# The order of TensorE's attention matmuls in the four middle blocks of an attention and two-layer MoE kernel: from a list schedule to the order of emission

## The chip, the cores and the metric

The kernel runs on one core of a Trainium2 chip. The metric is the device time of one execution in microseconds (us); lower is better. Five engines work in parallel, each through its own instruction stream in order: TensorE (PE) multiplies matrices, VectorE (DVE), ScalarE (ACT) and GpSimd (POOL) do elementwise work, SyncE (SP) issues DMAs. An instruction waits for what it needs, and everything behind it in its stream waits too.

## What is computed

Attention over q, k, v of shape (4, 8, 576, 64), then two feed-forward stages over 2304 tokens:

```python
def _attn_ref(q, k, v):
    ...
    out_d = sm_attn(q_d, k_d, v_d)          # q, k, v averaged over groups of 4 tokens
    out_up = np.repeat(out_d, factor, axis=2)
    mask = np.abs(pos[:, None] - pos[None, :]) < factor
    ...
    out_local = np.matmul(attn, v)          # softmax over the band |i - j| < 4
    return out_up + out_local

def _moe_ref(x, w_gate, w_val, w_out, rms_g):
    xn = x / rms * rms_g
    g = xn @ w_gate
    silu = g * (1.0 / (1.0 + np.exp(-g)))
    return silu * (xn @ w_val) @ w_out

def _moe2_ref(x, w_in, w_out, s, b):
    r = np.maximum(x @ w_in, 0.0)
    return (s * (r * r) + b) @ w_out
```

## The kernel before, in words

The 2304 tokens are cut into 8 **blocks** of 288. A block of the first feed-forward stage is `main(blk)`: 12 pairs of accumulations `pg` and `pvl` (gate and value), 12 matmuls of 128x288 each, then 4 output rows `po` of 36 matmuls each. The generator yields after every 12 matmuls, so a block has 36 **steps**. Before it, attention must be there: batch b of the attention gives blocks 2b and 2b+1. Blocks 0 and 1 run together (`main01`), while batch 1 of the attention is computed beside them. Batch 2 is computed beside blocks 2 and 3, batch 3 beside blocks 4 and 5. Blocks 6 and 7 run beside the preparation of the second stage's weights, and the second stage (`ph`, `y`) follows.

A batch of attention is four **units** (one pair of heads each), written as the generator `attn_unit`. In the before a new unit starts every `UNIT_STEP` = 10 steps of the block. A unit does, in this order: load `qkf` and `vd`, `vw` (q, k; v in groups of 4; v in windows); sums of squares and their sum over partitions on TensorE, `ss`; from it powers of two as scales (`pow2`); `qk`, high and low halves of q and k (ACT, then DVE); a DMA transpose to `qkT`, from which DVE copies `q_b`; `pd` (24 small matmuls on `qk`), its halves `qd` and six copies `qd_b`; `sd` (9 matmuls) and the softmax to `P_d`, whose DMA transpose is `PdT`; `sl` (27 matmuls, in two parts) on `q_b` and `qkT` and the softmax to `P_l`, whose DMA transpose is `PlT`; `vh` and `vdh`, halves of v (POOL, ACT, POOL); `pvd` (36 matmuls, waits for `PdT`), `pl` (30 and 24 matmuls, wait for `PlT` and `vh`), their sum into X, and squares into `sq_sum`. After the four units `norm` makes `ssn` and `rb` for each half of the batch and scales X.

Buffers couple the units. `qkf`, `qk`, `qkT`, `P_l`, `PlT` have one buffer each. `vd` and `vw` share one buffer (tag "vd"), so the order in which the code asks for them is the order in which they take turns. `ss`, `pd`, `sd`, `ssn` and `rb` share one PSUM buffer (tag "x"), `pvd` and `pl` another (tag "v"). The accumulations of `main` have four ("mm"), that is two pairs. All DMAs of the units go through SP's one stream.

In the before the framework's list schedule places each instruction of each engine by its priority and by when it holds it to be ready; `main` steps and one step of the attention are emitted in turn. So TensorE's stream splits the attention's matmuls and sets pieces of several units side by side.

Of the kernel before, what the change touches and what calls it, by code (L numbers as in the profile page):

```python
# [35 lines left out]
UNIT_STEP = 10  # L36
# [35 lines left out]
def kernel(  # L72
# [197 lines left out]

    def softmax_d(sd, scale, de=None):
        dm = ap.tile([128, 3], F32, tag="dm", name="dm", bufs=2)
        dz = ap.tile([128, 3], F32, tag="dz", name="dz", bufs=2)
        dve.tensor_reduce(out=dm, in_=sd, axis=AX.X, op=ALU.max)
        dve.tensor_scalar(out=dm, in0=dm, scalar1=scale, scalar2=-1.0, op0=ALU.mult, op1=ALU.mult)
        if de is None:
            de = ap.tile([128, 3, SD], F32, tag="de", name="de")
# [3 lines left out]
        return de, dz  # L281

# [24 lines left out]
    last = []  # L307
    gates = {}
# [195 lines left out]
    def attn_unit(b, hp, sq_sum):  # L504
# [7 lines left out]
        vs, sc, cs = stats(hp, qkf, vd, qk.bitcast(BF16).rearrange("p a b -> p (a b)"))  # L512
# [13 lines left out]
        yield  # L526
# [45 lines left out]
        yield

    def norm(b, hh, sq_sum):
# [15 lines left out]
        yield  # L590
# [16 lines left out]
        yield  # L607
# [179 lines left out]
    def attn_batch(b):  # L787
        sq_sum = ap.tile([128, S], F32, tag="sqsum", name="sqsum")
        if b == EARLY:
            clear()  # L790
        gens = [(early_unit if b < EARLY else attn_unit)(b, hp, sq_sum) for hp in range(NP)]
        step = UNIT_STEP if b >= EARLY else UNIT_STEP1 if b else UNIT_STEP0
# [266 lines left out]
```

## Time and profile before

| | |
|---|---|
| time, three runs | 1064.8, 1066.89, 1067.55 us (median 1066.89) |
| the profiled execution | 1066.8 us, span from first to last instruction 1065.1 us |
| PE busy | 988.2 us, 93% of the span |
| DVE, ACT, POOL busy | 597.1, 517.0, 323.9 us (56%, 49%, 30%) |
| chain that ended last, by engine | PE 62%, DVE 14%, DMA 12%, ACT 5%, issue 4% |

The page's slices show PE at 7 to 9 tenths of busy time between about 320 and 530 us and a granted clock of 8 tenths between about 290 and 370 us, where the middle blocks are. Busy shares of PE are of little use by themselves: matmuls are pipelined, their ends are modelled, and at half the clock the same matmul is busy twice as long. Waits and the granted clock are read instead.

### The profile page before, as it was taken

What the parts mean: (1) busy time and instruction counts of PE and PEld (TensorE: products, weight loads), DVE (VectorE), ACT (ScalarE), POOL (GpSimd) and SP (SyncE); (2) the same over time, 40 slices, a digit from 0 to 9 for tenths busy, and PEclk for the clock granted to TensorE, in tenths of its full rate; (3) what the DMA queues carried; (4) which work ended last, traced back from release to release, by engine and by line L of the source; (5) the groups of instructions that cost most, each with busy time, mean ns of one, the idle gap of its engine ahead of it and who ended that gap; (6) DMA issues with size and microseconds to landing.
All of it is one profiled execution on the core that took longest, in us unless ns stands there. A gap on an engine that the chain in (4) does not pass through costs nothing.

```text
span 1065.1 us, 20448 instructions
## 1 busy us (share of the span) xinstructions
PE 988.2 (93%) x8198; PEld 668.0 (63%) x8198; DVE 597.1 (56%) x1263; ACT 517.0 (49%) x1174; POOL 323.9 (30%) x417
## 2 busy tenths in 40 slices
PE   7975999999997799888899899999999999999998
PEld 4753777778765677666687677654555545455553
DVE  4798975363884764867826777574332414233240
ACT  3876686355644544555436777663321404132140
POOL 7433753245644355535542206420000000000000
PEclk9986999999988899999999999999999999999999
DMA  9985144010345430555312424300000000000000
GB/s 193 232 223 153 61 134 124 14 24 14 69 83 117 95 62 2 93 103 100 61 24 86 153 86 161 111 1 10 21 10 20 1 30 1 20 11 10 20 1 30
DMA packets 128111, 73.59 MB, mean 69 GB/s; under 512 B 111376, under 2 KB 115984, under 8 KB 128016
## 3 DMA queue, kind: packets, MB, share of 16 engines
q1 hardware_dynamic: 128016, 72.29, 26.9%
q8 instruction: 64, 1.05, 0.4%
q14 instruction: 31, 0.25, 0.1%
HBM read 54.97 MB, written 4.72 MB: 56 GB/s over the span
## 4 chain that ended last, share of the span: by engine, by line
PE 62%; DVE 14%; DMA 12%; ACT 5%; issue 4%; POOL 2%; SPq 1%; DVEq 0%; POOLq 0%; ACTq 0%
PE y L1021 18%; PE ph L1001 17%; PE po L737 8%; PE pg L716 7%; PE pvl L716 6%; DMA stg<-in_moe_w_in_dram 3%; DMA stg<-in_moe_w_out_dram 2%; DMA qkT<-qk 2%; DMA PlT<-P_l 2%; DVE W L638 2%; DVE stg L634 2%; PE pl L369 1%; DMA PdT<-P_d 1%; ACT stg L633 1%; DVE W L130 1%
## 5 line engine op out<-in xcount | busy, mean ns | idle before, releaser
L716 PEld LDWEIGHTS <-W 128*128 128x128 f16 x2304 | 227.5, 100 | 83.9 <-issue 20.7
L1001 PE MATMUL ph<-X,W 128*128 128x384 f16 x1152 | 196.6, 326 | 0.4 <-DVE s4o L681 0.3
L716 PE MATMUL pg<-X,W 128*128 128x288 f16 x1152 | 169.8, 295 | 9.5 <-DVE u L723 8.5
L716 PE MATMUL pvl<-X,W 128*128 128x288 f16 x1152 | 167.8, 292 | 4.8 <-DVE u L192 3.0
L1001 PEld LDWEIGHTS <-W 128*128 128x128 f16 x1152 | 112.6, 98 | 82.7 <-issue 3.3
L1021 PE MATMUL y<-W 128*128 128x512 f16 x648 | 151.6, 379 | 0.0
L737 PEld LDWEIGHTS <-W 128*128 128x128 f16 x1152 | 112.1, 99 | 36.2 <-issue 7.0
L737 PE MATMUL po<-g,W 128*128 128x288 f16 x1008 | 132.5, 289 | 1.0 <-POOL g L727 0.7
L1005 ACT ACTIVATE r<-ph 128x384 f32<-128x384 f32 x96 | 46.9, 489 | 176.1 <-PE ph L1001 126.6
L727 POOL TENSOR_TENSOR g<-u,g 128x288 f16<-128x288 f32 x84 | 73.5, 875 | 136.8 <-ACT g L726 136.8
L1021 PEld LDWEIGHTS <-W 128*128 128x128 f16 x648 | 63.4, 98 | 71.0
L192 DVE SCALAR_TENSOR_TENSOR r<-ph,r 128x384 f32<-128x384 f32 x96 | 53.5, 557 | 59.4 <-ACT r L1005 59.4
L1026 DVE SCALAR_TENSOR_TENSOR ys<-y,ccol,bcol 128x512 f32<-128x512 f32 x18 | 13.5, 751 | 121.1 <-PE y L1021 118.9
L726 ACT ACTIVATE g<-u 128x288 f16<-128x288 f32 x84 | 36.8, 438 | 60.8 <-DVE u L192 59.9
L634 DVE SCALAR_TENSOR_TENSOR stg<-stg 128x512 int32<-128x512 int32 (+1 forms) x53 | 40.3, 760 | 36.4 <-ACT stg L633 36.3
L1009 DVE TENSOR_TENSOR W<-r,W 128x384 f16<-128x384 f32 x72 | 40.1, 558 | 36.5 <-ACT W L1008 36.5
L723 DVE SCALAR_TENSOR_TENSOR u<-u,pvl 128x288 f32<-128x288 f32 x96 | 43.0, 448 | 26.9 <-PE pvl L716 22.2
L1008 ACT ACTIVATE W<-r 128x384 f16<-128x384 f32 x72 | 37.5, 521 | 40.0 <-DVE r L192 40.0
L722 ACT ACTIVATE u<-pg,tsc 128x288 f32<-128x288 f32 x96 | 46.9, 488 | 14.7 <-PE pg L716 13.6
L1021 PE MATMUL y<-W,r2b 128*128 128x512 f16 x216 | 50.0, 379 | 0.0
L192 DVE SCALAR_TENSOR_TENSOR u<-u,pg 128x288 f32<-128x288 f32 x96 | 43.1, 449 | 1.7
L632 ACT ACTIVATE W<-stg 128x512 f32<-128x512 f32 (+1 forms) x53 | 34.0, 644 | 20.3 <-DMA stg<-in_moe_w_out_dram 9.1
(266 smaller groups left out, 1427.1 us busy)
## 6 DMA issues: line engine op xcount, KB each, us to landing
stg<-in_moe_w_out_dram SPq DMA_DIRECT2D x25, 512.0 KB
stg<-in_moe_w_in_dram SPq DMA_DIRECT2D x16, 512.0 KB
out_dram<-ys SPq DMA_DIRECT2D x18, 256.0 KB
W<-in_moe_w_gate_dram SPq DMA_DIRECT2D x10, 384.0 KB
W<-in_moe_w_val_dram SPq DMA_DIRECT2D x10, 384.0 KB
qkf<-in_q_dram SPq DMA_DIRECT2D x26, 144.0 KB
qkf<-in_k_dram SPq DMA_DIRECT2D x26, 144.0 KB
vd<-in_v_dram SPq DMA_DIRECT2D x13, 288.0 KB
```

The source lines that it names most:

```text
L192: (eng or dve).scalar_tensor_tensor(out=o, in0=a, scalar=s, in1=b, op0=ALU.mult, op1=ALU.mult)
L634: ins = dve.scalar_tensor_tensor(out=stg[:, :, 0], in0=stg[:, :, 1], scalar=-2 ** 31, in1=stg[:, :, 0], op0=ALU.bitwise_and, op1=ALU.bitwi ...
L716: pe.matmul(out=acc, lhsT=Cgv.half(o, FP, lw)[:, f0 * 128:f0 * 128 + 128], rhs=X16[:, kc, 3 * blk:3 * blk + 3, lx, :], start=i == 0, stop= ...
L722: act.activation(out=u, in_=ps[0], func=AF.Tanh, scale=tsc[:, part:part + 1])
L723: dve.scalar_tensor_tensor(out=u, in0=u, scalar=1.0, in1=ps[1], op0=ALU.add, op1=ALU.mult)
L727: pool.tensor_tensor(out=lo, in0=u, in1=hi, op=ALU.subtract)
L737: pe.matmul(out=acc, lhsT=Co.half(fc * 512, 512, lw)[:, m * 128:(m + 1) * 128], rhs=g16(fc)[:, lx, :], start=i == 0, stop=i == 35)
L1001: pe.matmul(out=acc, lhsT=C2.half((p * KC + kc) * 512, 512, lw)[:, f0 * 128:f0 * 128 + 128], rhs=X16[:, kc, 4 * blk:4 * blk + 4, lx, :], s ...
L1005: act.activation(out=r, in_=acc, func=AF.Relu, scale=2.0 ** -23)
L1008: act.activation(out=dst[:, 0, :], in_=r, func=AF.Copy)
L1009: dve.tensor_tensor(out=dst[:, 1, :], in0=r, in1=dst[:, 0, :], op=ALU.subtract)
L1021: pe.matmul(out=y, lhsT=src[:, lx, tt * 128:(tt + 1) * 128], rhs=C3.half(fc * 512, 512, lw), start=i == 0, stop=i == 47)
```

## The change

The change sets TensorE's order in blocks 2 to 5 by hand: inside `tc.manual_schedule(engines={pe.engine})` its instructions stay in the order in which the code emits them. One step of `main` (12 matmuls) and one `tick()` of the attention alternate, and the attention's matmuls of a step stand together. Between its stages a unit now waits a number of steps, `lag(n)`. A unit starts every 12 steps. In a unit's own steps: `ss` at 6, `pd` at 10, `sd` at 13, `sl` at 15 and 16, `pvd` at 24, `pl` at 25 and 26. Batch 2 starts 14 steps before `main01` ends, batch 3 at step 66 of the 72 of blocks 2 and 3. The windows `vw` are asked for only after `P_l`, so `vw` of a unit takes its turn behind `vd` of the next. `qk` is made in two halves, q first. The squares follow each half of `pl`, and the norm of the first half no longer waits for the end of the batch. The other engines keep the list schedule.

```diff
-UNIT_STEP = 10
+UNIT_STEP = 12
+LAG_SS = 3
+LAG_PD = 4
+LAG_SD = 3
+LAG_SL = 2
...
+LAG_VH = 3
+LAG_V = 4
+LAG_RB = 3
+LAG_X = 2
+START2 = 60
+START3 = 66
...
     def attn_unit(b, hp, sq_sum):
-        vw = ap.tile([WIN, 2, NJ, D], F32, tag="vd", name="vw")
-        load_unit(b, hp, qkf, vd, vw)
-        yield
+        load_unit(b, hp, qkf, vd, None)
+        yield from lag(LAG_SS)
...
-        act.activation(out=qv[:, :, 0], in_=qkv, func=AF.Copy, scale=sc[:GR, 0:1])
-        dve.scalar_tensor_tensor(out=qv[:, :, 1], in0=qkv, scalar=sc[:GR, 0:1], in1=qv[:, :, 0],
-                                 op0=ALU.mult, op1=ALU.subtract)
+        for t in range(2):
+            act.activation(out=qv[:, t, 0], in_=qkv[:, t], func=AF.Copy, scale=sc[:GR, 0:1])
+            dve.scalar_tensor_tensor(out=qv[:, t, 1], in0=qkv[:, t], scalar=sc[:GR, 0:1], in1=qv[:, t, 0],
+                                     op0=ALU.mult, op1=ALU.subtract)
...
         sp.dma_start_transpose(out=PlT, in_=P_l.rearrange("p a b -> p (a b)"))
+        vw = ap.tile([WIN, 2, NJ, D], F32, tag="vd", name="vw")
+        load_windows(b, hp, vw)
+        yield from lag(LAG_VH)
...
         split_v(vs, vw, vdh, vh, sc)
-        yield
+        yield from lag(LAG_V)
         od = values_d(vdh, PdT, cs[:, 1:2])
...
+    def attn_later(b):
...
+            if gens and n % UNIT_STEP == 0:
+                live.append(gens.pop(0))
...
+                elif got == "half":
+                    halves_ += 1
+                    if halves_ == NP:
+                        live.append(later_norm(b, 0, sq_sum))
...
+    def middle(blk):
+
+        while (blk // 2, blk % 2) not in normed:
+            tick()
+        for n, _ in enumerate(main(blk)):
+            if n == 2:
+                run_posts()
+            if 36 * (blk - 2) + n == START3:
+                sides.append(attn_later(3))
+            tick()
...
+        if blk == 2:
+            with tc.manual_schedule(engines={pe.engine}):
+                for mid in range(2, NB - 2):
+                    middle(mid)
...
+            if blk == 0 and n >= START2:
+                if n == START2:
+                    drain(side)
+                    sides.append(attn_later(2))
+                tick()
```

Three places show the moved order. The first is TensorE's stream at the start of block 2, unit 0 of batch 2, before (`W_86` holds the weights; `ones_b`, `pool_m` are constants):

```order
L716 MATMUL pg<-X,W_86 128x288
L264 LDWEIGHTS ones_b
L264 MATMUL ss<-accb,ones_b 128x2
L716 LDWEIGHTS W_86
L716 MATMUL pvl<-X,W_86 128x288
...
L532 LDWEIGHTS qk
L532 MATMUL pd<-pool_m,qk 128x24
L716 LDWEIGHTS W_86
L716 MATMUL pvl<-X,W_86 128x288
```

And of the change, at the same place:

```order
L739 MATMUL pvl<-X,W_86 128x288
L282 LDWEIGHTS ones_b
L282 MATMUL ss<-accb,ones_b 128x2
L555 LDWEIGHTS qk
L555 MATMUL pd<-pool_m,qk 128x24
...
L310 LDWEIGHTS qd_b
L310 MATMUL sd<-qd,qd_b 128x144
L325 LDWEIGHTS q_b
L325 MATMUL sl<-qkT,q_b 128x70
```

Before, four accumulations of `main` (48 matmuls) and one matmul of a fifth stand between `ss` and the first `pd`, and another 45 matmuls of `main` between that `pd` and the first `sl`; in the change `ss`, the 24 `pd`, the 9 `sd` and the first 15 `sl` of this unit follow each other with nothing of `main` between. For the other units four steps of `main` stand between `ss` and `pd`, and five more between `pd` and `sl`.

The second place is SP's stream in batch 2, from `qkT` of unit 1 to that of unit 2, before:

```order
L520 DMA_TRANSPOSE qkT<-qk 128x24x96
L560 DMA_TRANSPOSE PlT<-P_l 128x18x128
L237 DMA qkf<-in_q_dram 96x6x64 x2
L237 DMA qkf<-in_k_dram 96x6x64 x2
L549 DMA_TRANSPOSE PdT<-P_d 128x12x128
L238 DMA vd<-in_v_dram 72x4x256
L560 DMA_TRANSPOSE PlT<-P_l 128x18x128
L240 DMA vw<-in_v_dram 70x2x64
L241 DMA vw<-in_v_dram 70x2x64
L244 DMA vw<-in_v_dram 70x7x64 x2
L520 DMA_TRANSPOSE qkT<-qk 128x24x96
```

And of the change:

```order
L543 DMA_TRANSPOSE qkT<-qk 128x24x96
L581 DMA_TRANSPOSE PlT<-P_l 128x18x128
L248 DMA qkf<-in_q_dram 96x6x64 x2
L248 DMA qkf<-in_k_dram 96x6x64 x2
L249 DMA vd<-in_v_dram 72x4x256
L256 DMA vw<-in_v_dram 70x2x64
L571 DMA_TRANSPOSE PdT<-P_d 128x12x128
L257 DMA vw<-in_v_dram 70x2x64
L260 DMA vw<-in_v_dram 70x7x64 x2
L543 DMA_TRANSPOSE qkT<-qk 128x24x96
```

In both, `PlT` of a unit stands behind `qkT` of the next one. In the change the `vw` that follows is that of unit 1, behind `vd` of unit 2, and there is one `PlT` between two `qkT`.

The third place is DVE's stream behind `ss` of unit 1 of batch 2 (`sqh`, `sqs`, `sqi` are the steps of `pow2`, `u` belongs to `main`), before:

```order
L186 TENSOR_SCALAR sqh<-ss 128x2
L547 SCALAR_TENSOR_TENSOR P_d<-de,dz,P_d 128x2x72
L187 TENSOR_SCALAR sqs<-sqh 128x2
L188 TENSOR_SCALAR sqi<-sqs 128x2
L192 SCALAR_TENSOR_TENSOR cs<-sqi 128x1
L268 TENSOR_SCALAR cs<-sqi 128x1
L557 TENSOR_TENSOR P_l<-ch,P_l 128x5x70
L723 SCALAR_TENSOR_TENSOR u<-u,pvl 128x288
L192 SCALAR_TENSOR_TENSOR u<-u,pg 128x288
L517 SCALAR_TENSOR_TENSOR qk<-qkf,sqs,qk 96x2x768
L557 TENSOR_TENSOR P_l<-ch,P_l 128x4x70
```

And of the change:

```order
L197 TENSOR_SCALAR sqh<-ss 128x2
L354 TENSOR_SCALAR z<-z 128x4
L198 TENSOR_SCALAR sqs<-sqh 128x2
L355 RECIPROCAL z<-z 128x4
L199 TENSOR_SCALAR sqi<-sqs 128x2
L203 SCALAR_TENSOR_TENSOR cs<-sqi 128x1
L286 TENSOR_SCALAR cs<-sqi 128x1
L746 SCALAR_TENSOR_TENSOR u<-u,pvl 128x288
L540 SCALAR_TENSOR_TENSOR qk<-qkf,sqs,qk 96x768
L203 SCALAR_TENSOR_TENSOR u<-u,pg 128x288
L540 SCALAR_TENSOR_TENSOR qk<-qkf,sqs,qk 96x768
L578 TENSOR_TENSOR P_l<-ch,P_l 128x5x70
```

`qk` now stands in two halves ahead of both `P_l`; before, the first `P_l` stood ahead of it.

## Rows read from the trace of the kernel before

**Rows 1.** Windows: us, busy time of each engine, granted PE clock, DMA

```profile
261.97:561.64 299.67, 266.79 (x3012) 209.21 (x3010) 195.00 (x457) 149.47 (x347) 148.00 (x173) 0.95 0.37 72
561.64:685.54 123.90, 113.85 (x894) 87.06 (x892) 90.29 (x167) 94.29 (x199) 41.96 (x43) 1.00 0.37 128
295.00:305.00 10.00, 8.99 (x98) 6.37 (x98) 6.38 (x13) 2.53 (x7) 3.27 (x4) 0.66 0.69 112
```

**Rows 2.** Waits of PE, 261.97 to 561.64: us in total, times, longest

```profile
PE pg L716 <- DVE u L723: 6.5, 4, 2.4
PE pl L369 <- DMA PlT<-P_l: 6.1, 4, 2.3
PE pvd L353 <- DMA PdT<-P_d: 4.9, 3, 2.6
...
PE pvl L716 <- DVE u L192: 2.0, 2, 1.8
```

**Rows 3.** Timeline of PE, block 2: start, us, instructions

```profile
261.97 1.63 PE L716 MATMUL pg<-X,W 128*128 128x288 f16 x12
...
266.50 0.17 PE L264 MATMUL ss<-accb,ones_b 128*128 128x2 bf16 x1
...
275.69 0.73 PE L532 MATMUL pd<-pool_m,qk 96*128 96x24 f16 x23
...
281.43 0.74 PE L287 MATMUL sd<-qd,qd_b 128*128 128x144 f16 x9 [0.36 <-DVE qd_b L539]
282.00 0.96 PE L302 MATMUL sl<-qkT,q_b 128*128 128x70 f16 x24
```

**Rows 4.** Chain that ended last, 250 to 412: start, us, what

```profile
274.96 4.84 DMA qkT<-qk
...
298.17 5.63 DMA qkT<-qk
...
361.69 6.55 DMA PlT<-P_l
...
368.29 0.66 PE pl L369 x30
...
378.74 0.67 PE pvd L353 x36
...
380.98 1.47 PE pg L716 x12
...
387.75 5.10 DMA PlT<-P_l
...
403.72 5.51 PE po L737 x45
```

**Rows 5.** Timeline of SP: start, us in SP's stream

```profile
358.66 2.93 SPq L520 DMA_TRANSPOSE qkT<-qk  x1
```

**Rows 6.** Groups by line, 261.97 to 561.64: busy, mean ns of one

```profile
L517 DVE SCALAR_TENSOR_TENSOR qk<-qkf,sqs,qk 96x1536 f16<-96x1536 f32 x8 | 15.0, 1876 | 2.1 <-ACT qk L516 2.1
L760 DVE SCALAR_TENSOR_TENSOR X<-xt,pos,X 128x288 f16<-128x288 f32 x16 | 12.3, 782 | 0.6 <-ACT X L759 0.6
L539 DVE COPY qd_b<-qd 64x128 f16<-64x128 f16 x48 | 11.9, 299 | 0.4
L524 DVE COPY q_b<-qkT 64x1152 f16<-64x1152 f16 x16 | 7.9, 491 | 12.3 <-DMA qkT<-qk 12.2
L192 DVE SCALAR_TENSOR_TENSOR cs<-sqi 128x1 f32<-128x1 f32 x8 | 7.8, 980 | 0.1
L187 DVE TENSOR_SCALAR sqs<-sqh 128x2 int32<-128x2 int32 x8 | 3.6, 456 | 0.1
L723 DVE SCALAR_TENSOR_TENSOR u<-u,pvl 128x288 f32<-128x288 f32 x48 | 21.5, 448 | 11.5 <-PE pvl L716 10.3 <-ACT g L726 0.7 <-ACT u L722 0.3
```

**Rows 7.** Timeline of PE behind two waits: start, us, instructions

```profile
325.93 6.21 PE L737 MATMUL po<-g,W 128*128 128x288 f16 x28
...
369.51 2.59 PE L716 MATMUL pg<-X,W 128*128 128x288 f16 x10
```

**Rows 8.** Timeline of all engines near 268: start, us, instructions

```profile
268.21 2.32 POOL L132 TENSOR_TENSOR vw<-vw,sqs 70x1152 f32<-70x1152 f32 x1
...
268.49 2.06 DVE L192 SCALAR_TENSOR_TENSOR cs<-sqi 128x1 f32<-128x1 f32 x1
```

More of the change, by code (lines that the diff above doesn't have):

```diff
@@ L239, in load_unit, with load_windows @@
                      in_=v[b, h0:h0 + 2].rearrange("h (t p r) d -> p (h t) (r d)", p=72, r=4))
+        if vw is not None:
+            load_windows(b, hp, vw)
+    def load_windows(b, hp, vw):
+        h0 = 2 * hp
         sp.dma_start(out=vw[:, :, 0, :], in_=v[b, h0:h0 + 2, 0:WIN, :].rearrange("h p d -> p h d"))
@@ L281, in softmax_d, with lag @@
         return de, dz
+    def lag(n):
+        for _ in range(n):
+            yield
     def scores_d(qd, cs):
@@ L307 @@
     last = []
+    normed = set()
     gates = {}
@@ L525, in attn_unit @@
         kT = qT[:, 1].rearrange("p (l s) -> p l s", l=2)
-        yield
+        yield from lag(LAG_PD)
         pd = pX.tile([128, 288], F32, tag="x", name="pd")
@@ L539, in attn_unit @@
                 dve.tensor_copy(out=qd_b[ph, :, o, 64 * h:64 * h + 64], in_=qd[ph, :, q0:q0 + 64])
-        yield
+        yield from lag(LAG_SD)
         de, dz = scores_d(qd, cs)
-        yield
         for o in range(3):
@@ L549, in attn_unit @@
         sp.dma_start_transpose(out=PdT, in_=P_d.rearrange("p a b -> p (a b)"))
-        yield
+        yield from lag(LAG_SL)
         for js in JS:
             sl = scores_l([q_b[:, 9 * l:9 * l + 9] for l in range(2)], [kT[:, l] for l in range(2)], js, mp)
-            yield
             a = softmax_l(sl, js, cs[:, 0:1], 2.0 ** -14, mp, pool if b <= AMPB else dve)
@@ L563, in attn_unit, with norm @@
         split_v(vs, vw, vdh, vh, sc)
-        yield
+        yield from lag(LAG_V)
         od = values_d(vdh, PdT, cs[:, 1:2])
         yield
-        for js in JS:
+        for hh, js in enumerate(JS):
             values_l(b, hp, js, vh, PlT, od, cs[:, 1:2])
-            yield
-        for hh in range(2):
             squares(b, hp, hh, sq_sum)
-        yield
-    def norm(b, hh, sq_sum):
+            yield ("half", None)[hh]
+    def norm(b, hh, sq_sum, l1=1, l2=1):
         ss = pX.tile([GR, 3], F32, tag="x", name="ssn")
@@ L589, in norm @@
                 pool.tensor_tensor(out=r, in0=r, in1=rp[i], op=ALU.subtract)
-        yield
+        yield from lag(l1)
         rb = pX.tile([128, TB], F32, tag="x", name="rb")
@@ L606, in norm @@
             gates[3] = tuple(last)
-        yield
+        yield from lag(l2)
+        normed.add((b, hh))
     ring = [W1[:, 15744 + 1024 * i:15744 + 1024 * i + 1024].bitcast(I32).rearrange("p (n t) -> p n t", t=2)
@@ L788, in attn_batch @@
         sq_sum = ap.tile([128, S], F32, tag="sqsum", name="sqsum")
[L789 to L792, printed above, removed]
+        gens = [early_unit(b, hp, sq_sum) for hp in range(NP)]
+        step = UNIT_STEP1 if b else UNIT_STEP0
         live = []
@@ L807, in attn_batch, with later_norm @@
             yield
-        if b >= EARLY:
-            yield from norm(b, 0, sq_sum)
         yield from norm(b, 1, sq_sum)
+    def attn_later(b):
+        sq_sum = ap.tile([128, S], F32, tag="sqsum", name="sqsum")
+        if b == EARLY:
+            clear()
+        gens = [attn_unit(b, hp, sq_sum) for hp in range(NP)]
+        live = []
+        n = halves_ = 0
+        while gens or live:
+            if gens and n % UNIT_STEP == 0:
+                live.append(gens.pop(0))
+            for g in list(live):
+                got = next(g, 0)
+                if got == 0:
+                    live.remove(g)
+                elif got == "half":
+                    halves_ += 1
+                    if halves_ == NP:
+                        live.append(later_norm(b, 0, sq_sum))
+            n += 1
+            yield
+        yield from later_norm(b, 1, sq_sum)
+    def later_norm(b, hh, sq_sum):
+        yield from lag(1)
+        yield from norm(b, hh, sq_sum, LAG_RB, LAG_X)
     def rest():
@@ L892, in drain, with tick @@
             pass
+    sides = []
+    def tick():
+        for g in list(sides):
+            if next(g, 0) == 0:
+                sides.remove(g)
+    def middle(blk):
[7 more added lines that the diff above has]
+            tick()
+        if blk == NB - 3:
+            while sides:
+                tick()
     W2 = C2 = None
```

12 lines of the change are left out of this document (9 added, 3 removed).

## The prediction

> **What bounds the kernel now.** I read the page first, then the windows, the waits of PE, the timeline of PE, the chain, and last the groups by line. The middle blocks, from the first `pg` of block 2 at 261.97 us to that of block 6 at 561.64, take 299.7 us [rows 1]. What TensorE needs there without a wait and at full clock can be put together. 45 `po` take 5.51 us in the chain [rows 4], so a matmul of `main` takes 0.1224 us and a step of 12 takes 1.47, which the chain shows too. A row of the timeline runs some 0.16 us into the next (1.63 for the same 12 matmuls [rows 3]). Four blocks of 432 matmuls make 211.6 us, 16 `sn` 2.0. A unit of attention needs about 0.6 for `pd`, 0.57 for `sd` (281.43 to 282.00), 0.9 for 27 `sl` [rows 3], 0.67 for `pvd`, and for 54 `pl` at 0.66 per 30 another 1.2 [rows 4]: 3.9 together, 31.4 for eight units. The norms are some 60 small matmuls; at half the price of one of `main`, an estimate, they make 3.6. The sum is 248.6, so **51.1 us are lost** in the stage, to waits and to the clock.
>
> Where they go: PE's waits name DVE's `u` (6.5 and 2.0 us), `PlT` (6.1) and `PdT` (4.9) first [rows 2]; no single one rules. Most of them are 1 to 3 us long, and they cost twice. The granted clock averages 0.95 in the stage and 0.66 between 295 and 305 us, a mix of the two levels 2.4 and 1.2 GHz [rows 1]. 28 `po` behind a pause took 6.21 - 0.16 = 6.05 us where 3.43 would do, 2.6 lost; 10 `pg` behind a wait for `PlT` took 2.43 instead of 1.22, 1.2 lost [rows 7]. So a small wait costs half as much again.
>
> **The change part by part.** No computation is removed or added: `qk` alone is split in two. The orders decide.
>
> *Start of block 2.* The first unit's steps 0 to 13 are emitted beside `main01`, but nothing of block 2 stands between its `ss`, `pd`, `sd` and `sl`, as TensorE's order shows. `ss` could not come much earlier than in the before, since it shares the buffer "x" with the norm of batch 1. So TensorE stands still while the scales and halves are made. In DVE's stream behind `ss`: seven small operations of the scales at some 0.2 each, an estimate under `sqs`, 1.4; `sqs` 0.46, `cs` 0.98, `u` 0.45, the two halves of `qk` 1.88 [rows 6]: 5.2 us, then `qkT` is issued and lands 4.84 to 5.63 later [rows 4], at 10.0 to 10.8. Meanwhile DVE does four X (3.1), `qd` (as a `u`, 0.45) and six `qd_b` (1.8) [rows 6], until 10.5, then the two `q_b` (1.0), and `sl` starts at 11.5. Work in there is 1.2, so 10.3 us are idle. Below: small operations at nothing and no X, 8.8. Above: `ss` to `qkT` took 266.50 to 274.96 in the before [rows 3, 4], 8.5 instead of 5.2, which makes 13.9. I take 10.3, as the X stand behind `qk` now. With 2.6 for the clock behind such a pause this is **12.9**. Before, this place was covered by nearly eight steps of `main`, and lost little.
>
> *Lag from `ss` to the next unit's needs.* A cycle of 12 steps needs 12 x 1.47 + 3.9 = 21.5 us. The tightest lag that I find is of two units: `PlT` of unit u is issued behind `qkT` of unit u+1 on SP. From `ss` of u+1 (its step 6) to `pl` of u (its step 25, which is step 13 of u+1) TensorE has 7 steps, a `pd` and a `pvd`: 11.6 us. The need: in DVE's stream five small operations 1.0, `sqs` 0.46, `cs` 0.98, two `u` 0.9, `qk` 1.88, together 5.2; `qkT` holds SP for 2.93 [rows 5]; then `PlT` lands 5.10 to 6.55 after its issue [rows 4]: 13.2 to 14.7. So `pl` waits 1.6 to 3.1 us, in six units (0 to 2 of each batch; the last has no `qkT` ahead). I take the middle, 2.3: **13.8**. Below: the small operations at nothing, 12.2, a wait of 0.6. Behind `PlT` in SP's stream stand `qkf` and `vd` of the next unit but one, and then `vw`; they come later by what it waits, and with a cycle of 24 instead of 21.5 they have the room. For half of the six I add 1.2 for the clock, **3.6**, with 0 and 7.2 as bounds.
>
> *The other lags.* `sd` to `pvd` has 11 steps, over 16 us, before `PdT`; its 4.9 us of waits should go. `pd` to `sd` has 3 steps, `pvd` and the first `pl`, 5.7 us, for `qd` and six `qd_b` (2.3 [rows 6]) behind `q_b`, which wait for `qkT`: it just fits, and a late `sd` delays what stands behind it only if `pl` has not delayed it already. The `u` waits of PE, 8.5 now, have the same four buffers; DVE is no longer held long by `q_b` ahead of `u`, so I take half, **4.2** (0 to 8.5). The last units' `pl`, `pl` behind the copy of `pvd` (one step) and the norms, 3 to 4 steps each, I put at **4** (0 to 8).
>
> *The sum:* 12.9 + 13.8 + 3.6 + 4.2 + 4 = 38.5 lost instead of 51.1, a gain of 12.6. The profiled execution took 1066.8 us, 1.7 more than its span, and the median of the runs is 1066.89. Forecast: 1066.8 - 12.6 = **1054 us**.
>
> *Behind the stage.* The norm of batch 3 now ends 44 matmuls of `main` earlier ahead of block 6, 5.4 us, and the preparation of the second weights, which takes over its memory, can start so much earlier. Blocks 6 and 7 take 123.9 us for 864 matmuls of `main` [rows 1], 105.8 by the rate; some of the rest waits for that preparation. I take nothing, since TensorE's list order moved the preparation's matmuls forward too; at most 5.
>
> **The rivals.** *The lags cover (1035).* If DVE reaches `qk` in 4.2 us and `PlT` lands in 5.1, `pl` waits 0.6, 3.6 in all; with 11.4 at the start and 4 for the rest 19 are lost, 32 less than now. For it: in the before many of these transfers were ready when TensorE came, and PE's waits sum to little for each cause [rows 2]. Against: 12.2 us are needed in 11.6 even then.
>
> *DVE stays as slow as before (1090).* GpSimd's work on v holds DVE: beside `vw` on POOL, 268.21 to 270.53, the `cs` of 128 numbers took 2.06 us and ended with it [rows 8], against a mean of 0.98 [rows 6]. If each unit meets this between `ss` and `qk`, as the 8.5 us of [rows 3, 4] contain it, the start loses 13.9 + 2.6, `pl` waits 8.5 + 2.93 + 5.1 to 6.55 - 11.6, that is 5.6 in the middle, 33.6 for six, the clock 1.9 (between 1.2 and 2.6) each, 11.4, `u` 8.5 and the rest 4: 74 us, 23 more than now. It decides from where the six units' wait and clock reach 51.1 - 12.9 - 8.2 = 30, 5.0 each, a wait of 3.8: when `ss` to `qkT` takes 6.7 us. Against it: `vw` now lands late in the cycle, behind `vd` of the next unit and a `PdT`, so POOL's long work falls behind `qk`, and `qk` stands ahead of `P_l`.
>
> The Trainium skill has this as a rule ("SBUF — State Buffer", section "Who interferes with whom"): DVE's second port is GpSimd's only one, an exclusive lock, and a DVE instruction with two SBUF inputs fully blocks while a GpSimd instruction that reads SBUF holds it. The row of `cs` agrees. By the rule alone both halves of `qk` and both `P_l` can lose a POOL instruction's length, which is the case above; by the rows' means, which contain the collisions of the before, it is the forecast.
>
> *No difference (1064 to 1070).* The start's idle time and waits near 3.8 us give back all that the longer lags save; it is the border of the case above.
>
> **How the numbers follow.** The forecast's case has 0.48 (1046 to 1062 by its own bounds), the covering lags 0.24, no difference 0.10, DVE as slow as before 0.18. About 0.3% (3.2 us) is what a measurement of this kernel can tell from no change. Faster than that: 0.72; within: 0.10; slower: 0.18. The range from 1030 to 1074 leaves out about 0.04 below and 0.15 above.
>
> **What would show it.** In the profile after: a hole of some 10 us in PE between the first `ss` and the first `sl` of block 2, waiting for DVE `qk` and `q_b`, with a low clock behind it; waits of `pl` for `PlT` of 1.6 to 3.1 us in six units and few others; waits for `PdT` nearly gone; `ss` to `ss` some 24 us. The forecast is wrong if the hole is much shorter, if `vh` (POOL) and not `PlT` releases `pl`, if waits of `sd` for `qd_b` come on top, or if the blocks 6 and 7 change by more than 5 us.

## The result and the profile after

The changed kernel takes 1075.05 us (median; 1068.89 for the kernel before in the same comparison), a ratio of 1.0051 with a 95% interval of 1.0027 to 1.0075: it is 0.5% slower, where 1054 was forecast. One execution of 1669 us is left out of the ratio as disturbed. The profiled execution took 1077.7 us, its span 1076.0.

The windows of the changed kernel, first the middle blocks, then blocks 6 and 7 (columns as in [rows 1]):

```profile
267.73:574.37 306.64, 265.70 (x3011) 209.37 (x3009) 198.69 (x470) 155.14 (x361) 147.24 (x177) 0.95 0.36 70
574.37:697.17 122.80, 113.61 (x898) 87.53 (x896) 88.01 (x164) 92.05 (x195) 42.05 (x40) 1.00 0.38 129
```

The middle blocks take 306.64 us against 299.67 [rows 1], 58.0 more than the work of 248.6 instead of the 38.5 forecast. Blocks 6 and 7 are as they were. Block 2 begins 5.8 us later than in the profile before (267.73 against 261.97), though TensorE's order is the same up to there; eight kernels with the same start of batch 2 begin it between 260.5 and 266.1, so most of this is the difference of one execution from another. What the change does lies in the stage.

PE's waits in the stage, after (us in total, times, longest), to be held against [rows 2]:

```profile
PE pg L739 <- DVE u L746: 7.5, 6, 2.7
PE pl L393 <- ACT od L382: 7.5, 2, 4.2
PE pl L393 <- DMA PlT<-P_l: 5.6, 3, 2.0
PE pd L555 <- DVE qk L540: 4.9, 7, 1.3
PE pvl L739 <- DVE u L746: 3.6, 1, 3.6
PE pl L393 <- ACT vdh L144: 3.0, 1, 3.0
PE sd L310 <- DVE qd_b L562: 2.7, 1, 2.7
PE pd L555 <- ACT qk L539: 2.4, 1, 2.4
PE po L760 <- POOL g L750: 1.6, 1, 1.6
```

The waits for `PdT` are gone, as forecast. The `PlT` waits are there, 1.7 to 2.0 us each, but three instead of six, and one of them is of unit 3, where none was forecast. The wait put down to `vdh`, which `pl` does not read, is a fourth one for `PlT`: it ends 4.74 us behind the issue of `PlT`, as the waits at 362.76 and 388.31 do (4.73 and 4.69), and 0.3 us behind the end of `od`, where the two waits of `od` end 0.05 us behind it.

```profile
461.78 2.69 SPq L581 DMA_TRANSPOSE PlT<-P_l  x1
...
465.86 0.36 ACT L382 ACTIVATE od<-pvd,cs 128x144 f32<-128x144 f32 x1
...
466.13 0.40 ACT L144 ACTIVATE vdh<-vs 72x256 f16<-72x256 f32 x1
...
466.52 0.66 PE L393 MATMUL pl<-PlT,vh 70*64 70x64 f16 x30 [3.03 <-ACT vdh L144]
```

In the two other units where `pl` waits, a cause stands in front that had been put with the small terms: `od`, the copy of `pvd`. The timeline of all engines in unit 0 of batch 2, in order of time, shows how (start, us, instruction, idle time before it):

```profile
295.82 3.31 DVE L578 TENSOR_TENSOR P_l<-ch,P_l 128x350 f16<-128x350 f32 x2
...
296.30 2.96 SPq L543 DMA_TRANSPOSE qkT<-qk  x1
...
296.45 2.38 POOL L143 TENSOR_TENSOR vw<-vw,sqs 70x1152 f32<-70x1152 f32 x1
...
301.11 0.74 PE L377 MATMUL pvd<-PdT,vdh 72*64 72x64 f16 x36
...
301.89 2.36 POOL L145 TENSOR_TENSOR vh<-vw,vh 70x1152 f16<-70x1152 f32 x1 [0.61 <-ACT vh L144]
...
302.94 2.10 DVE L547 COPY q_b<-qkT 64x1152 f16<-64x1152 f16 x2 [1.68 <-DMA qkT<-qk]
...
305.05 0.81 DVE L562 COPY qd_b<-qd 64x128 f16<-64x128 f16 x6
...
305.89 0.46 DVE L746 SCALAR_TENSOR_TENSOR u<-u,pvl 128x288 f32<-128x288 f32 x1
306.38 0.45 DVE L203 SCALAR_TENSOR_TENSOR u<-u,pg 128x288 f32<-128x288 f32 x1
...
306.87 0.44 ACT L749 ACTIVATE g<-u 128x288 f16<-128x288 f32 x1 [4.66 <-DVE u L203]
307.21 0.36 ACT L382 ACTIVATE od<-pvd,cs 128x144 f32<-128x144 f32 x1
...
307.63 1.01 PE L393 MATMUL pl<-PlT,vh 70*64 70x64 f16 x30 [4.20 <-ACT od L382]
```

Read from the bottom: `pl` waits for `od`, a copy of 0.36 us whose input was there 5 us before. `od` stands behind a `g` in ACT's stream, `g` waits for `u`, and `u` stands in DVE's stream behind `q_b`, which waits for `qkT` of the next unit. So three streams in order tie the `pl` of one unit to the `qkT` of the next. And twice on the way GpSimd's work lies beside a DVE instruction: the two `P_l` take 3.31 us while POOL has `vw`, and the two `q_b` 2.10 while it has `vh`, where [rows 6] has 491 ns for one.

### The profile page after: what moved, and what is told of

The parts are those of the page before. It is cut to its first block, busy times and chain, and to the rows that moved or that the text cites. A ratio compares the mean times of both kernels' runs of the same rounds, so it can differ in the third digit from the quotient of the medians.

```text
span 1076.0 us, 20478 instructions
## 1 busy us (share of the span) xinstructions
PE 992.3 (92%) x8198; PEld 672.4 (62%) x8198; DVE 598.2 (56%) x1271; ACT 520.6 (48%) x1182; POOL 323.5 (30%) x417
## 3 DMA queue, kind: packets, MB, share of 16 engines
HBM read 54.97 MB, written 4.72 MB: 55 GB/s over the span
## 4 chain that ended last, share of the span: by engine, by line
PE 43%; DMA 5%; DVE 4%; ACT 2%; issue 1%; POOL 0%; SPq 0%; DVEq 0%; ACTq 0%; POOLq 0%
PE y L1098 17%; PE ph L1078 17%; PE po L760 4%; DMA stg<-in_moe_w_out_dram 2%; DMA stg<-in_moe_w_in_dram 2%; PE pg L739 2%; PE pvl L739 2%; DVE W L661 1%; ACT stg L656 1%; DVE stg L657 1%; DMA PlT<-P_l 0%; ACT W L655 0%; PE pl L393 0%; DVE P_d L569 0%; DVE u L746 0%
## 5 line engine op out<-in xcount | busy, mean ns | idle before, releaser
L739 PE MATMUL pg<-X,W 128*128 128x288 f16 x1152 | 169.5, 297 | 13.9 <-DVE u L746 12.8
L750 POOL TENSOR_TENSOR g<-u,g 128x288 f16<-128x288 f32 x84 | 70.1, 835 | 122.5 <-ACT g L749 122.2
L745 ACT ACTIVATE u<-pg,tsc 128x288 f32<-128x288 f32 x96 | 47.0, 490 | 16.4 <-PE pg L739 11.7
L657 DVE SCALAR_TENSOR_TENSOR stg<-stg 128x512 int32<-128x512 int32 (+1 forms) x53 | 39.8, 752 | 25.7 <-ACT stg L656 25.4
L661 DVE SCALAR_TENSOR_TENSOR W<-W,stg 128x512 int32<-128x512 int32 (+1 forms) x53 | 42.5, 805 | 2.6 <-ACT W L655 2.0
```

The source lines that it names most:

```text
L657: ins = dve.scalar_tensor_tensor(out=stg[:, :, 0], in0=stg[:, :, 1], scalar=-2 ** 31, in1=stg[:, :, 0], op0=ALU.bitwise_and, op1=ALU.bitwi ...
L661: dve.scalar_tensor_tensor(out=di, in0=di, scalar=3, in1=stg[:, :, 0], op0=ALU.logical_shift_left, op1=ALU.bitwise_or)
L739: pe.matmul(out=acc, lhsT=Cgv.half(o, FP, lw)[:, f0 * 128:f0 * 128 + 128], rhs=X16[:, kc, 3 * blk:3 * blk + 3, lx, :], start=i == 0, stop= ...
L745: act.activation(out=u, in_=ps[0], func=AF.Tanh, scale=tsc[:, part:part + 1])
L750: pool.tensor_tensor(out=lo, in0=u, in1=hi, op=ALU.subtract)
```

## The experiments

All are run against the kernel before on one chip for each set of four; 1% is 10.7 us. "Blocks 2 to 6" is the time from the first `pg` of block 2 to that of block 7 in the profiled execution, and "idle" that stretch up to block 6 less PE's busy time there. Two of these kernels are told apart when their ratios differ by more than about 0.3%. (In the kernels with the later `pl` a last piece of the norm and 24 `po` fall behind the first `pg` of block 6; therefore blocks 2 to 6 are compared.)

| kernel | ratio to before | 95% interval | blocks 2 to 6, us | idle, us |
|---|---|---|---|---|
| before | 1 | | 363.3 | 32.9 |
| the change (fixed order) | 1.0051 | 1.0027–1.0075 | 368.9 | 40.9 |
| e1_od | 1.0035 | 1.0021–1.0049 | 366.7 | 35.2 |
| e2_start | 0.9992 | 0.9973–1.0012 | 364.3 | 37.1 |
| e3_vw_dve | 0.9996 | 0.9973–1.0019 | 365.6 | 36.3 |
| e5_pl_late | 1.0031 | 1.0010–1.0052 | 365.6 | 35.9 |
| e6_pl_late_start | 0.9954 | 0.9933–0.9976 | 360.0 | 32.4 |
| e15_fixed_start_vw_dve | 0.9936 | 0.9908–0.9963 | 358.3 | 33.4 |
| e12_fixed_all | 0.9880 | 0.9862–0.9898 | 352.4 | 27.1 |
| e13_fixed_all_sd | 0.9894 | 0.9865–0.9922 | 353.3 | 26.9 |
| e11_fixed_vw_early | 1.0225 | 1.0207–1.0243 | 390.8 | 58.0 |
| e4_list | 0.9907 | 0.9888–0.9926 | 349.8 | 24.6 |
| e7_list_vw_early | 0.9977 | 0.9959–0.9996 | 361.1 | 31.1 |
| e8_list_qk_whole | 0.9939 | 0.9922–0.9957 | 354.6 | 26.3 |
| e9_list_start | 0.9898 | 0.9870–0.9927 | 353.1 | 26.8 |
| e10_list_vw_dve | 0.9846 | 0.9826–0.9866 | 346.9 | 19.8 |
| e14_list_start_vw_dve | 0.9905 | 0.9890–0.9920 | 349.8 | 26.4 |
| e16_before_vw_dve | 0.9860 | 0.9830–0.9890 | 349.7 | 22.6 |

**First set: one suspect each.** The edits to the changed kernel:

```diff
 e1_od
-LAG_V = 4
+LAG_V = 2
         od = values_d(vdh, PdT, cs[:, 1:2])
-        yield
+        yield from lag(3)
 e2_start
-START2 = 60
+START2 = 68
 e3_vw_dve (in split_v, the halves of vw)
-        halves(..., vw.rearrange("p h j d -> p (h j d)"), sc[:WIN, 1:2], pool)
+        halves(..., vw.rearrange("p h j d -> p (h j d)"), sc[:WIN, 1:2], dve)
 e4_list
-            with tc.manual_schedule(engines={pe.engine}):
+            with nullcontext():
```

> The changed kernel with `pvd` two steps earlier (step 22 of its unit) and three steps of `main` instead of one between `pvd` and the first `pl`; `pl` stays at its step. Theory A (the copy of `pvd` to `od` stands in ACT's stream behind a `g` that waits for `u`, which in DVE's stream waits behind `q_b` for `qkT`, and one step is too short for that): the three waits of `pl` for `od` (4.2, 3.3, 3.0 us) and the clock behind them (some 1.2 each) go, so 8 to 14 us less than the changed kernel, and no `pl` waits over 1 us for `od`. Theory B (DVE is late in the cycle whatever stands on it, so the wait is only renamed): `pl` waits as long for `PlT`, or `pg` for `u`, at the same places; 0 to 3 us less.

Theory B. The waits for `od` are gone, and at the same places `pl` now waits for `PlT`, in all 14.0 us for 16.1; the ratio's interval overlaps that of the change. PE's waits of `pl`:

```profile
PE pl L393 <- DMA PlT<-P_l: 11.8, 5, 3.4
...
PE pl L393 <- ACT g L749: 2.2, 1, 2.2
```

(The wait put down to `g` ends 4.72 us behind the issue of its `PlT` and is one for `PlT` too.) So `od` and `PlT` are two things that are late by about the same; taking one away uncovers the other.

> The changed kernel with batch 2 begun 8 steps later beside `main01` (step 68 instead of 60), so that its `pd`, `sd` and `sl` of unit 0 are emitted inside block 2 with 4, 3 and 2 steps of `main` between, as in the other units. Theory A (the start of block 2 loses 11.6 us because nothing of `main` stands between them): first `ss` to second `ss` loses under 3 us, and the kernel is 8 to 12 us faster than the changed one. Theory B (DVE's stream of that stretch is late also beside `main`, so `pg` and `sl` wait there): some 5 us faster, with `u`, `q_b` or `qk` waits of 4 us or more in total in that stretch. If the start costs nothing in the end, because the batch ends later: within 3 us.

The place went as theory A has it: first `ss` at 268.19, second at 289.25, 21.1 us for 12 steps (17.6) and `pd`, `sd`, `sl` (2.1), so 1.3 lost where the change lost 11.7 (below). But only 0.6% (6.3 us) of these 10 came out at the end: later in the stage PE waits more for `od` (9.0 for 7.5), `u` (13.6 for 11.1) and `g` (4.8 for 2.0).

> The changed kernel with the halves of the windows `vw` made by ACT and DVE, as those of `qk` are, and not by POOL, ACT, POOL: two POOL instructions of 2.3 us a unit go, DVE gets one of some 1.5 us more. Theory A (GpSimd's work holds DVE, and so makes `q_b`, `qk` and `u` late): `ss` to `qkT` falls from 7.3 to 10.9 us towards 6, PE's waits fall by a third or more, 5 to 12 us faster than the changed kernel. Theory B (DVE's own queue is what is late): 1.5 us more on DVE in each unit, within 3 us of the changed kernel or up to 6 slower.

Theory A in size (0.55%, 5.9 us), and for what DVE does; `ss` to `qkT` fell less than it said (below), and PE's idle time by 4.6 us, a ninth and not a third. DVE and POOL groups in the stage (busy us, mean ns of one), after:

```profile
L547 DVE COPY q_b<-qkT 64x1152 f16<-64x1152 f16 x16 | 10.7, 669 | 8.8 <-DMA qkT<-qk 8.7
L578 DVE TENSOR_TENSOR P_l<-ch,P_l 128x280 f16<-128x280 f32 x8 | 9.6, 1201 | 1.6 <-ACT P_l L577 1.6
L578 DVE TENSOR_TENSOR P_l<-ch,P_l 128x350 f16<-128x350 f32 x8 | 9.1, 1138 | 0.3 <-ACT P_l L577 0.3
...
L145 POOL TENSOR_TENSOR vh<-vw,vh 70x1152 f16<-70x1152 f32 x8 | 19.9, 2486 | 5.3 <-ACT vh L144 5.3
L143 POOL TENSOR_TENSOR vw<-vw,sqs 70x1152 f32<-70x1152 f32 x8 | 18.6, 2320 | 9.3 <-DMA vw<-in_v_dram 9.3
```

and in e3_vw_dve:

```profile
L141 DVE SCALAR_TENSOR_TENSOR vh<-vw,sqs,vh 70x1152 f16<-70x1152 f32 x8 | 11.4, 1423 | 2.0 <-ACT vh L140 1.9
...
L547 DVE COPY q_b<-qkT 64x1152 f16<-64x1152 f16 x16 | 7.7, 482 | 17.0 <-DMA qkT<-qk 16.9
...
L578 DVE TENSOR_TENSOR P_l<-ch,P_l 128x350 f16<-128x350 f32 x8 | 4.6, 574 | 1.2 <-ACT P_l L577 1.2
...
L578 DVE TENSOR_TENSOR P_l<-ch,P_l 128x280 f16<-128x280 f32 x8 | 3.7, 464 | 1.0 <-ACT P_l L577 1.0
```

The `P_l`, which nothing was done to, take 574 and 464 ns instead of 1138 and 1201. DVE has eight instructions more, 11.4 us, and is busy 187.2 us instead of 198.7: some 22.9 us of its busy time in the stage (11.4 + 11.5) were time in which GpSimd held it, as far as these durations tell. What is left over is `PlT`: 15.4 us in seven waits, where the change shows 5.6 in three.

> The changed kernel without the manual order: same lags, same late `vw`, same halves of `qk`, but TensorE's order in blocks 2 to 5 is that of the list schedule. Theory A (the fixed order puts `pl` one step behind `pvd` and loses by head-of-line waits): the list schedule spreads them and it is 5 to 12 us faster than the changed kernel. Theory B (the new lags and the late `vw` cost, not the fixed order): within 3 us of the changed kernel, with PE's waits on the same causes. If the fixed order brings something that the rest hides: over 3 us slower than the changed kernel.

Theory A, and more: 1.4% below the change and 0.9% below the kernel before. With the same lags the list order has 24.6 us of idle PE instead of 40.9, and no wait of `pl` over 0.9 us: between `pvd` and `pl` of a unit stand 14 to 110 matmuls of `main` instead of 12, and groups are split (in unit 0 of batch 2 one `pd`, then 10 matmuls of `main`, then the other 23 `pd`).

**Second set: can the fixed order be mended, and what of the change helps the list order?** e5 and e6 start from the change, e7 and e8 from e4_list:

```diff
 e5_pl_late; e6_pl_late_start has START2 = 68 too
         od = values_d(vdh, PdT, cs[:, 1:2])
-        yield
+        yield from lag(3)
 e7_list_vw_early
-        load_unit(b, hp, qkf, vd, None)
+        vw = ap.tile([WIN, 2, NJ, D], F32, tag="vd", name="vw")
+        load_unit(b, hp, qkf, vd, vw)
...
-        vw = ap.tile([WIN, 2, NJ, D], F32, tag="vd", name="vw")
-        load_windows(b, hp, vw)
 e8_list_qk_whole
-        for t in range(2):
-            act.activation(out=qv[:, t, 0], in_=qkv[:, t], ...)
+        act.activation(out=qv[:, :, 0], in_=qkv, ...)
```

> The changed kernel with `pvd` where it is and three steps of `main` instead of one before the first `pl`, so that both halves of `pl` come two steps (2.9 us) later. Theory A (a `pl` in a fixed order stops TensorE for the later of `od` and `PlT`, and both are 2 to 4 us late): the waits of `pl`, 16.1 us in the changed kernel, fall under 5, and the low clock behind them goes in part; 10 to 18 us less than the changed kernel. Theory B (the delay is handed on: with a later `pl`, its buffers `vh`, `PlT` and the PSUM of `pvd` come free later and the next unit's `pvd` or `PlT` wait instead): 0 to 5 us less.

The waits of `pl` fall from 16.1 us to 1.9 as in theory A, the time by 0.2%, which cannot be told from nothing: theory B. Where it went:

```profile
PE sd L310 <- DVE qd_b L562: 8.5, 4, 3.2
PE pg L739 <- DVE u L746: 6.8, 6, 2.8
PE pd L555 <- DVE qk L540: 6.4, 7, 2.3
PE po L760 <- ACT g L749: 3.2, 1, 3.2
```

`sd`, which had profited from a late `pl`, now waits itself, for the same late DVE.

> The same later `pl`, and batch 2 begun at step 68 of `main01` instead of 60 as well. Theory A (the waits of `pl` and the start of block 2 are two separate losses of the fixed order): both gains add, 5 us beside that of the later `pl` alone, and the fixed order comes to some 1055, near the list schedule with the same lags (1059). Theory B (any fixed order loses, since the waits move on to `u` and `qk`): no more than 6 us faster than the changed kernel in all.

Theory A by the sum (0.97% below the change; the start alone 0.59%, the later `pl` alone 0.20%), but not to the 1055 that it named.

> The list schedule with the new lags (1059.2), but `vw` asked for and loaded with its unit, ahead of `ss`, as before the change. It tells what the late `vw` is worth. Theory A (the late `vw` takes GpSimd's long work out of the stretch from `ss` to `qk`, and that is what makes the list schedule with the lags faster than before): back to 1066 to 1070. Theory B (the lags and the longer unit step of 12 do it): within 3 us of 1059.

Theory A: 0.70%, 7.5 us, of what the list order has over before come with the late `vw`; the lags and the split without it are worth 0.2%. With `vw` early `qk`'s halves take 1374 ns each, with the late `vw` 1122: POOL's work lay beside them.

> The list schedule with the new lags and the late `vw`, but `qk` made in one piece of q and k by ACT and then DVE, as before the change. In two halves DVE's first half runs beside ACT's second, so `qkT` should come about 1 us earlier with the split. If the split counts: 2 to 5 us slower than 1059. If there is time between `ss` and `pd` anyway: within 2 us of 1059.

The split counts, but barely clear of noise: 0.3% (3.4 us). How is not shown: DVE's two halves cost more than the whole (2 x 1122 ns against 1876 [rows 6]), and from `ss` to `qkT` the six units behind the first of each batch take 7.9 us in the mean with the split and 7.8 without.

**Third set.** e10 and e14 are e4_list with the line of e3, e14 with START2 = 68 as well; e11 is the change with the early `vw` of e7; e12 is the change with the edits of e5, e2 and e3 together.

> The list schedule with the new lags (1059.2) and the halves of `vw` made by ACT and DVE instead of POOL, ACT, POOL. With the fixed order this gave 6 us (1069.0 against 1075) and DVE's busy time in the middle blocks fell from 198.7 to 187.2 us although it got eight instructions more. Theory A (DVE held by GpSimd is what is left in the list order too): another 4 to 8 us faster, 1051 to 1055. Theory B (the list order has room for a late DVE, since `main` stands ahead of the attention's matmuls): within 3 us of 1059.

Theory A: another 0.6%. It is the lowest ratio of all, 0.9846.

> The changed kernel, fixed order and all lags, but `vw` asked for and loaded with its unit as before the change, so that `vd` of the next unit waits until `vh` of this one is made, at its step 20, the next unit's step 8. Theory A (the late `vw` is what makes a fixed order with these lags possible): `ss`, placed at step 6, waits for `accb` in six units, 3 to 6 us each, and the kernel is 15 to 40 us slower than the changed one. Theory B (`vw` early costs as in the list schedule, where it made 8 us): 5 to 10 us slower.

Theory A: `ss` waits for `accb` 28.0 us in five units, 9.2 the longest. The late `vw` is what lets the fixed order exist with these lags.

> The fixed order with three repairs: `pl` two steps later, batch 2 begun at step 68, and the halves of `vw` on ACT and DVE. Apart they gave 3.4, 6.2 and 6.0 us against the changed kernel, the first two together 11.3. Theory A (they are separate losses): 1057 to 1060, the same as the list schedule with the lags. Theory B (the remaining waits, `sd` for `qd_b` and `po` and `pg` for `g` and `u`, are no matter of GpSimd): 1062 to 1065.

Theory A: measured 1.71% against 0.59 + 0.20 + 0.55 = 1.34% for the three alone, a difference that the intervals do not tell from nothing. The fixed order is 1.2% below the kernel before.

> The list schedule with the lags, the halves of `vw` on ACT and DVE, and batch 2 begun at step 68. In the list order `main` stands between the first unit's matmuls anyway, so the later start should change nothing against the same kernel with the start at 60: within 2 us. If the later start pushes the batch's end into block 4: 2 to 6 us slower.

Neither as expected: 0.6% slower than e10, 6.8 us by the medians. Its stage is only 2.9 us longer (287.5 for 284.6); block 2 begins at 270.79 instead of 260.52, though TensorE's order is the same up to there. Part of this is one execution against another: the profiled one of e14 is the slowest of its seven (1064.83, median 1060.42), that of e10 the fastest of its five (1050.62, median 1053.66). What does the rest stays open.

**Fourth set: what was still open.** e9 is e4_list with START2 = 68; e13 is e12 with LAG_SD = 4 and LAG_SL = 1; e15 is e12 without the later `pl`; e16 is the kernel before with the one line of e3.

> The list order with the lags (0.9907 of the kernel before) and batch 2 begun at step 68 instead of 60. Theory A (the later start costs the list order something, as the kernel with the start and `vw` on DVE was 0.6% slower than that with `vw` on DVE alone): 0.995 to 0.999. Theory B (that difference had another cause, or goes with `vw`): 0.988 to 0.993.

Theory B: 0.9898, as e4_list. The later start by itself costs the list order nothing, so e14's loss had another cause.

> The fixed order with the three repairs (0.988) and `sd` a step of `main` later behind `pd`, `sl` at its place. Theory A (the four waits of `sd` for `qd_b`, 5.1 us, are a loss of their own): they go, 0.982 to 0.985. Theory B (what is late is DVE's stream, and the wait moves to `sl`, `pg` or `PdT`): 0.986 to 0.990.

Theory B: the waits of `sd` fall from 5.1 to 0.4 us, while those for `PlT` rise from 1.2 to 5.8 and those for `u` from 9.6 to 11.7; the two ratios can't be told apart.

> The fixed order with the later start and `vw` on ACT and DVE, `pl` one step behind `pvd` as in the change. Alone the two gave 0.59% and 0.55% of the changed kernel's 1.0051. Theory A (the later `pl` counts only once the rest is repaired, since with `vw` on DVE `pl` waited 15.4 us for `PlT`): 0.994 to 0.997, some 0.7% above the 0.988 with the later `pl`, with 13 us or more of waits for `PlT`. Theory B (the later `pl` is worth little here too): 0.988 to 0.991.

Theory A, a little under its range: 0.9936, 0.56% above the kernel with the later `pl`. Now the term of the forecast stands there in full:

```profile
PE pl L393 <- DMA PlT<-P_l: 13.1, 7, 3.1
...
PE pl L393 <- ACT od L382: 3.1, 1, 3.1
```

> The kernel before with nothing but the halves of `vw` on ACT and DVE. Theory A (GpSimd's work holds DVE in the kernel before as much as after the change, so it is no loss of the change): 0.993 to 0.997. Theory B (before, `vw` ran beside less of DVE's long work, or the list order covered it): 0.998 to 1.003.

More than theory A: 0.9860, a gain of 1.4% from one line in the kernel before, without any new order or lag. DVE is busy 186.3 us in the stage instead of 195.0 [rows 1] with 12.8 us of `vh` more, and PE idle 22.6 instead of 32.9.

```profile
264.90:549.22 284.32, 261.70 (x3012) 207.05 (x3009) 186.29 (x468) 151.18 (x352) 115.75 (x161) 0.98 0.39 76
```

What became shorter here is not `q_b` (505 ns for 491) but `qd_b` (208 for 299), X (586 for 782) and `cs` (526 for 980), held against [rows 6].

## Why the prediction was wrong

The forecast was 38.5 us lost in the stage; 58.0 were. The difference of 19.5 has two parts: PE's busy time beyond the work is 265.7 - 248.6 = 17.1 us where the terms for the clock had 2.6 + 3.6 = 6.2, and its idle time is 40.9 where the terms for waits had 10.3 + 13.8 + 4.2 + 4 = 32.3. Of the idle time the start has 8.1, `PlT` 8.6, `u` 11.1, and what had been put with the small terms 12.9 (`od` 7.5, `pd` for `qk` 3.4, `po` for `g` 2.0).

- **The sum, "38.5 lost instead of 51.1"**, is the first step that failed, by 10.9 us, and what was mis-sized in it are above all the terms for the clock. The trace records the granted clock: of PE's busy time in the stage 29.2 us were at 1.2 GHz before, 25.7 in the change and 13.7 in e4_list. A matmul takes about twice as long there (12 `pg` in 3.08 us, below), so half of that is what the clock cost: 14.6, 12.9 and 6.9 us. The sum gave the change 6.2, and it has 12.9, hardly less than before. It has six such stretches: 10.2 us in the start, and five of 3.4 or 6.8 us at the two waits of `od`, at the `PlT` wait of 466.52, at one of `u` and one of `po`; at the three `PlT` waits of 1.7 to 2.0 us there is none. What is left beyond the work, 3.6, 4.2 and 6.6 us, is work that the sum of 248.6 counts too low, or lies in the modelled ends of the matmuls; it was in the 51.1 too. Against idle time alone (32.9 before) the same terms of waits, 32.3, would have said "no difference".
- **The start of block 2** was about right: 12.9 forecast. From `ss` at 270.79 to `ss` at 288.97 are 18.2 us, with 6.5 of work (three steps, 4.4, and `pd`, `sd`, `sl`, 2.1), so 11.7 lost (8.1 of idle time for 10.3, and 3.6 of busy time beyond the work for 2.6), with the waits named and one of `sd` for `qd_b`:

```profile
270.79 0.17 PE L282 MATMUL ss<-accb,ones_b 128*128 128x2 bf16 x1
273.37 0.19 PE L555 MATMUL pd<-pool_m,qk 96*128 96x24 f16 x1 [2.41 <-ACT qk L539]
...
278.66 1.26 PE L310 MATMUL sd<-qd,qd_b 128*128 128x144 f16 x9 [2.69 <-DVE qd_b L562]
281.39 1.06 PE L325 MATMUL sl<-qkT,q_b 128*128 128x70 f16 x15 [1.47 <-DVE q_b L547]
282.25 3.08 PE L739 MATMUL pg<-X,W 128*128 128x288 f16 x12
...
288.97 0.17 PE L282 MATMUL ss<-accb,ones_b 128*128 128x2 bf16 x1
```

  The `pg` behind it takes twice its 1.47 us. e2_start shows that the place is the cause; that all of it comes back when it is mended is not so.
- **"`pl` waits for `PlT`, 13.8"** was right as a lateness and shows in full only once nothing stands in front: 8.6 us in the change (5.6 and the 3.0 put down to `vdh`), 14.0 in e1_od (11.8 and 2.2), 13.1 and 15.4 in e15 and e3, where seven units wait and not six.
- **"`pl` behind the copy of `pvd` (one step)"**, put with others at 4, took 7.5 us alone, in two waits for `od`. I had looked at the distance from `pvd` to `pl`, not at what is queued ahead of `od` on ACT, and ahead of that on DVE. It adds little to the time by itself (e1_od), since `PlT` is late at the same places.
- **`u`, 4.2** (0 to 8.5), is the term of waits that was most mis-sized: it measured 11.1 (7.5 + 3.6). And `pd` for `qk`, put at nothing outside the start, has 3.4, `po` for `g` 2.0: DVE is late everywhere.
- **"`ss` to `qkT` in 5.2 us"** is the assumption behind these, and it failed by 3.3 us. In the first unit of each batch it takes 4.7 and 4.3 us, in the six others 7.0 to 10.9, 8.5 in the mean (7.3 in the one shown, from 288.97 to 296.30). The forecast counted DVE's work from `sqh` on, as if DVE were free when `ss` comes. In the six, DVE starts `sqh` 0.8 to 4.5 us behind the start of `ss`, 2.5 in the mean, since pieces of softmax (`ch`, `z`, `P_d`) stand ahead of it in DVE's stream. The longest case:

```profile
503.94 0.17 PE L282 MATMUL ss<-accb,ones_b 128*128 128x2 bf16 x1
...
504.25 1.04 DVE L351 TENSOR_TENSOR ch<-ch,z 128x350 f32<-128x350 f32 x1
...
508.48 0.15 DVE L197 TENSOR_SCALAR sqh<-ss 128x2 int32<-128x2 int32 x1
```

  From `sqh` to `qkT` it is 6.0 us in the mean. In e12_fixed_all, without GpSimd's work on `vw`, that part is 5.2, as forecast; but the part ahead of `sqh` is 3.3 there, and the whole 8.5 again (8.4 in e15, 7.3 in e3). So GpSimd is the smaller part of this lateness, and what stands ahead of `sqh` the larger; no run took that away.
- **The rival "DVE stays as slow as before"** named 6.7 us for the same stretch as the point from which it decides, and 8.5 is beyond it, though mostly for another reason than the one it gave. It was dismissed because "POOL's long work falls behind `qk`". It does, but for two units (a half of `qk` took 2.5 us beside `vw` at 325.00 and 512.30), and then it lies beside `P_l` and `q_b`, which stand ahead of `u` and hold it. The rule of the Trainium skill weighed there ("SBUF — State Buffer", section "Who interferes with whom") agrees: both `P_l`, with two SBUF inputs, are the instructions that doubled against e3. The rival's own figure, 74 us lost, was too much: the terms that it adds up lie partly beside one another.
- **`ss` to `ss`** is 31.3, 27.9, 30.0 and 25.8 us where both units run in a fixed cycle, not 24; of the signs named for the forecast this one failed, and that of `PlT` waits in six units and few others. The signs named for its being wrong did not come: `vh` releases no `pl`, the one wait of `sd` for `qd_b` lies inside the hole, which is 10.6 us long, and blocks 6 and 7 changed by 1.1 us. **Behind the stage** there is nothing (122.8 for 123.9), and the `PdT` waits are gone.

What the change brings and takes is told apart by the list order. Its lags, late `vw` and split `qk` are good for 0.9% (e4_list), nearly all of it through `vw` (e7) and the split (e8). The fixed order takes 1.4% back, as every group that is late stops TensorE. Three mends of it (start, later `pl`, `vw` away from GpSimd) give 1.7%, and the ratio is then the one forecast (0.9880; 1054 against 1066.8 is 0.988), by repairs that the forecast did not have. But e16 and e10 cannot be told apart (0.9860 and 0.9846): with GpSimd's long work gone the kernel before needs neither the lags nor the order. These two have the lowest ratios of all. That GpSimd's work on `vw` costs 0.6, 0.6 and 1.4% is shown by e3, e10 and e16; that it costs by holding DVE rests on DVE's durations. The same line also shortens the way to `vh` (GpSimd, ACT, GpSimd becomes ACT, DVE) and takes some 36 us of work from GpSimd in the stage (147.2 to 111.4 in e3), and neither was tried apart from the hold. PE's waits name GpSimd once in the change, 1.6 us for `g`, and once in the kernel before:

```profile
PE ss L264 <- POOL accb L261: 3.0, 1, 3.0
```

That the fixed order's remaining 0.3% against e10 (e12) is DVE's lateness is only argued, from its waits.

## What to carry to other kernels

Before an order or lags are changed, look for the instruction whose mean duration differs most from its shortest, and for what runs beside it on another engine; here one line that took 4.8 us of GpSimd work per unit away from beside DVE was worth more than a new order of all matmuls. In a fixed order a lag has to cover not the chain of the data alone but all that stands ahead of each link in its engine's stream. Mending one late link uncovered the next here (e1, e5, e13), and the stream of the engine has to be read from the moment when the engine is free, not from the moment when the data is there. A forecast by a list of losses should be made for idle time and for busy time apart, with the cost of the clock as a term of its own, or what the change does not give back is counted as gain.

## What the runs showed of the hardware

Copies are held too: `q_b`, one SBUF input, takes between 451 and 1627 ns in the change, with its four longest (832 to 1627) beside `vh` and `vdh` on GpSimd, and 482 in the mean without GpSimd's work on `vw`. And the granted clock can fall without a pause: from 150 to 180 us TensorE is busy all the time in both of these kernels, whose orders are the same there, and the granted clock is 1.00 in e10 (first) and 0.89 in e14 (second), where it falls to the lower of its two levels at 163.4 us, 22 us behind the last pause of TensorE of over 0.1 us:

```profile
150.00:180.00 30.00, 29.97 (x265) 22.48 (x263) 20.30 (x43) 21.65 (x56) 10.28 (x14) 1.00 0.45 135
```

```profile
150.00:180.00 30.00, 30.00 (x248) 21.71 (x246) 20.30 (x39) 22.58 (x61) 9.82 (x12) 0.89 0.52 153
```

The second has 17 matmul records fewer in the same 30 us. Such differences ahead of block 2 may be part of why 29 executions of the kernel before lie between 1063.8 and 1077.1 us (not shown); stages are therefore compared here beside the times.
